# Seven products instead of eight for two more column groups of the projection and two more pairs of the second layer, and block sums taken from the transposes' banks

## The chip, the core and the metric

The kernel runs on one core of a Trainium2 chip. The metric is the time of one execution on the device, in microseconds (us): the median of 3 runs. The text calls TensorE PE (PEld is its weight load), VectorE DVE, ScalarE ACT, GpSimd POOL, and the engine that issues the transfers SP.

## What is computed

One transformer block on 2048 tokens of width 576: attention and a two-layer network stand side by side on the same normalized input, and both are added to `x`.

```python
def _A_ref(x, wqkv, wo):            # H = 32 heads of 18, W = 8 keys, every second token
    qkv = (lambda x, *d: x.transpose(*d))((x @ wqkv).reshape(B, S, 3, H, Dh), 2, 0, 3, 1, 4)
    ...
    logits = jnp.where(mask[None, None, :, :], logits, -1e9)
    attn = _softmax(logits, axis=-1)
    o = jnp.einsum("bhsw,bhswd->bhsd", attn, vg)
    return (lambda x, *d: x.transpose(*d))(o, 0, 2, 1, 3).reshape(B, S, D) @ wo

def _B_ref(x, w1, b1, w2):          # width F = 4608 between the layers, Mish
    h = jnp.einsum("bsd,df->bsf", x, w1) + b1
    ...
    return jnp.einsum("bsf,fd->bsd", act, w2)

xn = _layernorm(x, axis=-1)
return x + _A_ref(xn, A_wqkv, A_wo) + _B_ref(xn, B_w1, B_b1, B_w2)
```

## The kernel before, in words

**Number format.** Every operand of a matmul is split into a high part (a rounded copy, made by ACT) and a low part (the operand less its high part, made by DVE or POOL). A product of two operands is three matmuls: high by high, low by high, high by low. "Cast" is below the making of a high part, "low" that of a low part.

**Halves and blocks.** The tokens are worked off in two halves of 1024 (`hf`), each in two blocks of 512 (`b`), each of four tiles of 128 tokens (`jj`). Width 576 is four chunks of 128 and a rest of 64, which is stored twice. For each half come, in this order: normalization and transposition into the tiles `xt0` and `xt1` (`ln_transpose`, `transpose_split`: PE transposes into banks of PSUM, ACT and DVE split out of them); the projection to queries, keys and values in four column groups `g` of 432 columns; the two layers in 18 quads `q` of 256 hidden columns. The attention over the finished projection runs beside the quads on POOL, DVE and ACT, in 73 steps a half. The output projection by `wo` closes the program.

**Eight products or seven.** A product of 2 by 2 blocks takes eight block products, or seven if sums of blocks are made first. The sums of the input blocks are S1 to S4 (in the tiles `S0`, `S1`, `S2`, and S3 in place of A21), the differences of the weight blocks T1 to T4. Seven products were in use before in the first layer throughout (`m1_part`), in groups 2 and 3 of the second half (`z_part`, L502 to L577, 50 matmuls of 432 columns for each `jj`), in the second layer of the second half for `2 * OC` = 10 of its 18 quads (`p_item`, L949, seven items of 24 matmuls of 288 columns for two quads), and in the output projection. Groups 2 and 3 of the first half went through `qkv_item` (L416): 14 matmuls for each `g`, `b` and `jj`. The other eight quads of the second layer's second half went through `m2_cols` (L975): four chunks of 24 matmuls for each quad. The weight differences for the second half were prepared in the first: those of the second layer by `t_sum`, `t_high`, `t_low`, `t_keep` in quads 1 to 10, those of the projection by `z_load`, `z_sum`, `z_high`, `z_low`, `z_keep` from quad 10 on; both are written to DRAM and fetched later.

**Block sums.** `s_step` (L723) makes S1 to S4 on POOL, with three operations of 128x512 for S1 in each half of the columns `c`: A21 + A22 of the high parts, of the low parts, and the sum of the two.

**Order.** `plan` is a list of PE items; `add` appends one, `before(i, fn)` puts side work in front of item `i`, and each engine runs its instructions in the order in which the code issues them. Where the work stands is written by hand; the tables `MOVED`, `SUMS`, `AHEAD` shift single pieces of it, and `STEPS` holds the item at which each attention step stands. A tile waits for the readers of the buffer that it takes over. PSUM has four banks under the tag `h` and four under `out`.

**Start.** `first_item` interleaves the first four projection items with the transposes of their own tiles; its `mid` makes the root of tile 2's variance (ACT), then DVE's Newton step, then tile 3's statistics.

## Time and profile before

| | |
|---|---|
| median of 3 runs | 1104.5 us (1103.47, 1104.5, 1105.23) |
| the profiled execution's own time | 1103.77 us |
| its span (first to last instruction) | 1102.0 us |
| ACT busy | 503.7 us (46%), 927 instructions |
| DRAM traffic | read 162.16 MB, written 111.77 MB, mean 249 GB/s |
| matmuls of `qkv_item` (L439) | 672 of 432 columns |
| matmuls of `m2_cols` (L982) and `p_item` (L961) | 768 and 840 of 288 columns |

The page gives each engine's busy time, then the span in 40 slices, then the chain of waits, followed back from the last instruction. A window is a stretch of the span with each engine's busy time in it. A line of the timeline has the start, the duration, the engine, the code line, the tiles and, in brackets, the idle time before it with its releaser.

### The profile page before, as it was taken

The numbers are of one execution on the slowest core, as the hardware profiler recorded it, in microseconds if no ns is written. First come the engines' busy times: TensorE is split into PE (matmuls) and PEld (weight loads), VectorE is DVE, ScalarE is ACT, GpSimd is POOL, SyncE is SP. The second block draws the span as 40 slices with busy tenths as digits, with TensorE's granted clock in tenths as the row PEclk, the third lists the DMA queues.
The fourth block names the chain that finished last, engine by engine and source line by source line (L and its number), as shares of the span: only waits on it lengthen the run. The fifth ranks groups of instructions, "written<-read, shape, count | busy, mean of one in ns | idle before, by whom it ended". The sixth has DMA issues, their size and how long they took to land.

```text
span 1102.0 us, 18226 instructions
## 1 busy us (share of the span) xinstructions
PE 1095.1 (99%) x6526; PEld 1010.7 (92%) x6526; DVE 864.6 (78%) x1381; ACT 503.7 (46%) x927; POOL 800.9 (73%) x647
## 2 busy tenths in 40 slices
...
GB/s 204 283 312 302 256 344 224 249 264 261 259 281 211 287 252 306 260 257 227 171 307 301 226 337 341 241 218 221 207 240 185 180 219 201 239 309 198 250 218 139
DMA packets 181933, 275.12 MB, mean 250 GB/s; under 512 B 53426, under 2 KB 123860, under 8 KB 181844
## 3 DMA queue, kind: packets, MB, share of 16 engines
...
HBM read 162.16 MB, written 111.77 MB: 249 GB/s over the span
## 4 chain that ended last, share of the span: by engine, by line
PE 97%; DVE 1%; ACT 1%; POOL 0%; DMA 0%; issue 0%; SPq 0%; POOLq 0%
PE h L769 31%; PE po L869 21%; PE pq L439 11%; PE po L961 10%; PE po L982 9%; PE h L775 6%; PE o L1165 5%; PE z L537 4%; POOL act L821 0%; PE ta L163 0%; DMA acc<-in_x 0%; DVE st L200 0%; DVE accP L985 0%; PE tt L163 0%; DVE xt L170 0%
## 5 line engine op out<-in xcount | busy, mean ns | idle before, releaser
L869 PEld LDWEIGHTS po<-w,act 128*128 128x128 f32 x1728 | 236.3, 188 | 5.7 <-POOL act L821 0.4
L869 PE MATMUL po<-w,act 128*128 128x288 f32 x1728 | 240.6, 295 | 0.1
L627 POOL TENSOR_TENSOR pr<-q,kv 128x576 f32<-128x576 f32 x128 | 195.8, 1556 | 7.9 <-DMA q<-q_d 5.3
L666 POOL TENSOR_TENSOR pv<-L,kv 128x576 f32<-128x576 f32 x128 | 177.7, 1488 | 23.5 <-DVE L L659 12.9
L821 POOL TENSOR_TENSOR act<-c,act 128x512 fp32r<-128x512 f32 x75 | 103.2, 1376 | 113.0 <-ACT act L820 100.2
L439 PE MATMUL pq<-wq,xt 128*128 128x432 f32 x672 | 136.1, 360 | 0.9 <-ACT xt L169 0.6
L873 DVE TENSOR_TENSOR acc<-po,acc 128x288 f32<-128x288 f32 x288 | 117.2, 447 | 23.1 <-PE po L869 21.9
L439 PEld LDWEIGHTS pq<-wq,xt 128*128 128x128 f32 x672 | 125.0, 188 | 7.5 <-ACT xt L169 1.3
L961 PEld LDWEIGHTS po<-pw,u 128*128 128x128 f32 x840 | 114.9, 188 | 2.9 <-issue 0.2
L961 PE MATMUL po<-pw,u 128*128 128x288 f32 x840 | 116.8, 294 | 0.0
L815 ACT ACTIVATE c<-c,b1c 128x512 f32<-128x512 f32 x75 | 54.4, 725 | 129.4 <-DVE c L814 129.2
L769 PE MATMUL h<-xt,t 128*128 128x512 f32 x432 | 110.6, 391 | 0.2 <-DVE c L814 0.2
L769 PE MATMUL h<-S,t 128*128 128x512 f32 x432 | 110.4, 391 | 0.0
L982 PEld LDWEIGHTS po<-w,act 128*128 128x128 f32 x768 | 104.5, 188 | 2.7 <-DVE accP L985 0.7
L982 PE MATMUL po<-w,act 128*128 128x288 f32 x768 | 106.4, 295 | 0.1
L769 PE MATMUL h<-xt,wa 128*128 128x512 f32 x432 | 103.9, 389 | 0.0
L632 DVE TENSOR_REDUCE L<-pr 128x64 f32<-128x1152 f32 x64 | 85.6, 1340 | 19.6 <-POOL pr L627 19.5
L672 DVE TENSOR_REDUCE og<-pv 128x144 f32<-128x1152 f32 x64 | 85.9, 1344 | 18.6 <-POOL pv L666 18.6
L769 PEld LDWEIGHTS h<-xt,wa 128*128 128x128 f32 x432 | 80.9, 188 | 16.6
L803 ACT COPY c<-h 128x512 f32<-128x512 f32 x75 | 43.9, 586 | 108.2 <-PE h L775 62.2
L769 PEld LDWEIGHTS h<-xt,t 128*128 128x128 f32 x432 | 79.0, 188 | 15.3 <-DVE rt L814 0.5
L769 PEld LDWEIGHTS h<-S,t 128*128 128x128 f32 x432 | 77.9, 188 | 13.2 <-ACT rm L803 0.5
...
## 6 DMA issues: line engine op xcount, KB each, us to landing
...
```

Of the source, the lines that this page charges most:

```text
L439: nc.tensor.matmul(pq[:, 0:432], XT[:, xi, tok], wt[wi][:, hl, 0:432], start=i == 0, stop=i == len(seq) - 1)
L627: nc.gpsimd.tensor_tensor(out=pr[:, x:x + hh], in0=q[:, j0 + x:j0 + x + hh, None, :].to_broadcast([P, hh, W, CU]), in1=win(kt, 0, CU, j0 + ...
L632: nc.vector.tensor_reduce(L[:, k, j0:j0 + hj].rearrange("p j w h -> p (j w h)"), pr.rearrange("p j w (h d) -> p (j w h) d", h=2), axis=AX, ...
L666: nc.gpsimd.tensor_tensor(out=pr[:, x:x + hj].rearrange("p j d w -> p j w d"), in0=L[:, k, x:x + hj, :, h:h + 1].to_broadcast([P, hj, W, DH]),
L672: nc.vector.tensor_reduce(og[:, c0:c0 + DH, :].rearrange("p d j -> p j d"), pr, axis=AX, op=ALU.add)
L769: nc.tensor.matmul(ph, wt[:, wl, wk * P:(wk + 1) * P], X[:, xs, :], start=first and i == 0, stop=last and i == len(seq) - 1, skip_group_ch ...
L775: nc.tensor.matmul(ph, wt[:, wl, off * P:(off + 1) * P], X[:, xs, :], start=False, stop=wl == 1, skip_group_check=True)
L821: nc.gpsimd.tensor_tensor(out=a[:, 1, :], in0=t, in1=a[:, 0, :].bitcast(F32), op=ALU.subtract)
L869: nc.tensor.matmul(po, acts[hf, q, b, j][:, al, tok], done["w2", hf, 2 * q + j][:, wl, c * HC:(c + 1) * HC], start=i == 0, stop=i == 5)
L873: nc.vector.tensor_tensor(out=t, in0=po, in1=t, op=ALU.add)
L961: nc.tensor.matmul(po, units[e, k, qq][:, al, tok], w[:, qq, wl, :], start=i == 0, stop=i == 5)
L982: nc.tensor.matmul(po, acts[hf, q, b, j][:, al, tok], done["w2", hf, 2 * q + j][:, wl, c * HC:(c + 1) * HC], start=i == 0, stop=i == 5)
```

## The change

Five things are edited, and the order tables are written anew.

1. **Projection, first half, groups 2 and 3.** The 16 items of `qkv_item` go. In their place stand 14 items `y` (`za_part`), product by product in the order of `YORDER`: B11, B21, T2, T3, T4, T1, B22, each in two items of two `jj`. The last item of B22 stands inside quad 0, where the last `qkv_item` stood. The products that use B11, T2, T1 and B22 add up in one bank for each `jj` (four `out` banks for the whole stretch), B21 takes the four `h` banks, and T3 with T4 takes them over. ACT copies an intermediate state out of a bank, DVE adds another product to it. The raw weights (`za_load`) and their differences (`za_sum`, now on DVE) are made here; casts, lows and the way to DRAM (`za_high`, `za_low`, `za_keep`) too, for 16 tiles. So `z_load` to `z_keep` in quads 10 to 12 go. Block sums S1 to S3 of the first half are needed in this stretch, and their steps move ahead of it. The attention of the first half begins behind it.
2. **Second layer, second half.** `OC` goes from 5 to 6: twelve quads by `p_item`, six by `m2_cols`. `t_sum` to `t_keep` run for quads 11 and 12 too.
3. **A21 + A22.** `transpose_split` of block 1 has DVE add up the pairs in the bank, straight into the sum's tile; the three POOL operations for each `c` go, in both halves.
4. **Start.** The first half of tile 3's statistics stands between tile 2's root and its Newton step.
5. **Small moves.** The first block's products of the first chunk of quad 0 use the high parts first; the table for Mish is loaded in the projection; the loads of the second half's `x` stand six items later, the preparation of `wo` starts one quad further on and is spread over fewer items.

```diff
-OC = 5
+OC = 6
...
-STEPS = ((21, 22, 24, 26, 28, 30, 33, 38, 50, 51, 59, 61, 69, 71, 79, 81, 89, 92, 99, 104, 109, 110, 119, 121, 126, 128, 129,
...
+STEPS = ((36, 41, 47, 49, 53, 57, 63, 67, 70, 77, 78, 83, 85, 91, 95, 98, 105, 107, 111, 117, 123, 127, 130, 137, 139, 143,
...
+        if both is not None:
+            nc.vector.tensor_reduce(both, ta.rearrange("p (j k t) -> p k t j", j=2, k=2), axis=AX, op=ALU.add)
...
+    def half_stats(n, t):
+        if n not in half_st:
+            half_st[n] = sb.tile([P, 2, 6], F32, tag="st", bufs=4, name=f"st_{next(tpn)}"), []
+        st, ins = half_st[n]
+        c = len(ins)
+        ins.append(nc.vector.bn_stats(st[:, c, :], t[:, c * 288:(c + 1) * 288]))
...
+                half_stats(3, accs[0][3])
...
+        both = None
+        if b:
+            c, at_ = divmod(jj, 2)
+            if not at_:
+                s0[hf, c] = s_tmp(0)
+            both = s0[hf, c][:, :, at_ * P:(at_ + 1) * P]
+        transpose_split(xn, XTs[hf, b], jj * P, rem if b else None, (hf, b) == (1, 0) and jj < 3, both)
...
+    YHOME = {"B11": ("wb", "wb"), "B21": ("wb", "wc"), "R2": ("wc",), "R3": ("wc",), "T2": ("r3", "a0"),
+             "T3": ("a0", "a0"), "T4": ("a1", "a1"), "T1": ("a0", "a0"), "B22": ("a0", "a1")}
...
+    def za_sum(name, k):
...
-        nc.gpsimd.tensor_tensor(out=zraw[name, k], in0=zraw[x, k], in1=zraw[y, k], op=ALU.subtract)
+        nc.vector.tensor_tensor(out=zraw[name, k], in0=zraw[x, k], in1=zraw[y, k], op=ALU.subtract)
...
+    YORDER = ("B11", "B21", "T2", "T3", "T4", "T1", "B22")
...
+        to, add_ = {"B11": ((2, 0), 0), "B21": ((2, 0), 1), "T2": ((2, 1), 0), "T3": ((3, 1), 0), "T4": ((2, 1), 1),
+                    "T1": ((3, 1), 1), "B22": ((3, 0), 0)}[name]
...
+            if name == "B11":
+                yq["h1", jj] = ps.tile([P, 512], F32, tag="out", bufs=4, name=f"y1_{jj}")[:, 0:432]
+            elif name in ("B21", "T3"):
+                yq["h3", jj] = ps.tile([P, 512], F32, tag="h", bufs=4, name=f"y{name}_{jj}")[:, 0:432]
+            h = yq["h3" if name in ("B21", "T3", "T4") else "h1", jj]
+            seq = [(src[:, xs + k, tok], yw[name, k][:, wl]) for k in range(2) for xs, wl in ((hi, 0), (lo, 0), (hi, 1))]
+            if rest is not None:
+                seq += [(rest[0][:, rest[1], tok], yw[rest[2], 0][:, wl]) for wl in range(2)]
+            for i, (l, r_) in enumerate(seq):
+                nc.tensor.matmul(h, l, r_, start=i == 0 and name in ("B11", "B21", "T3"), stop=i == len(seq) - 1,
+                                 skip_group_check=True)
+            for d, v in ((kvs[:, :, jj, :], h[:, 0:288].rearrange("p (u c) -> p u c", u=2 * UQ)),
+                         (qs[:, :, jj, :], h[:, 288:432].rearrange("p (u c) -> p u c", u=UQ))):
+                if add_:
+                    nc.vector.tensor_tensor(out=d, in0=v, in1=d, op=ALU.add)
+                else:
+                    nc.scalar.copy(d, v)
...
-        t = stmp[k] = s_tmp(k)
-        if k == 0:
-            u = s_tmp("u")
-            gp(t, p["A21"][0], p["A22"][0], ALU.add)
-            gp(u, p["A21"][1], p["A22"][1], ALU.add)
-            gp(t, t, u, ALU.add)
-        elif k == 1:
+        t = stmp[k] = s_tmp(k) if k else s0[hf, c]
+        if k == 1:
             gp(t, stmp[0], p["A11"][0], ALU.subtract)
             gp(t, t, p["A11"][1], ALU.subtract)
         elif k == 2:
             gp(t, p["A12"][0], stmp[1], ALU.subtract)
             gp(t, t, p["A12"][1], ALU.add)
-        else:
+        elif k == 3:
...
-            for g, b in ((2, 0), (2, 1), (3, 1), (3, 0)):
-                for jj in range(JB - 1 if (g, b) == (3, 0) else JB):
-                    qi(hf, g, b, jj)
+            for n in range(len(YORDER)):
+                for half in range(2):
+                    if (n, half) != (len(YORDER) - 1, 1):
+                        yi(n, half)
...
+    z0 = at["y", 0, 0]
+    for name, k, lead in (("B11", 0, 12), ("B11", 1, 12), ("B12", 0, 11), ("R2", 0, 11), ("B21", 0, 10), ("B22", 0, 10),
+                          ("B21", 1, 9), ("B12", 1, 8), ("B22", 1, 8)):
+        before(z0 - lead, lambda name=name, k=k: za_load(name, k))
+    before(z0 + 1, lambda: za_load("R3"))
+    for name, k, d in (("T3", 0, -5), ("T1", 0, -5), ("T2", 0, -4), ("T3", 1, -1), ("T1", 1, -1), ("T2", 1, 0), ("T4", 0, 0),
+                       ("T4", 1, 1)):
+        before(z0 + d, lambda name=name, k=k: za_sum(name, k))
+    for name, k, d in (("B11", 0, -4), ("B11", 1, -3), ("B21", 0, -2), ("B21", 1, -1), ("R2", 0, -1), ("T2", 0, -3), ("T2", 1, 1),
+                       ("T3", 0, 1), ("T3", 1, 1), ("T4", 0, 2), ("T4", 1, 2), ("R3", 0, 5), ("T1", 0, 8), ("T1", 1, 8),
+                       ("B22", 0, 9), ("B22", 1, 10)):
+        before(z0 + d, lambda name=name, k=k: za_high(name, k))
+        before(z0 + d + (name[0] != "B" or name == "B22"), lambda name=name, k=k: za_low(name, k))
+        before(z0 + d + 4, lambda name=name, k=k: za_keep(name, k))
+    plan[z0 + 2][1].append(lambda: nc.scalar.preload_act_table_set("mish"))
...
-    i = spot(0, 2 * OC, 6)
...
-    i = spot(1, 2 * OC + 3, 0)
+    i = spot(1, 2 * OC + 2, 0)
...
-        k = i + 10 + (2, 5, 8, 12, 15, 19, 23, 27, 31)[n]
+        k = i + 8 + (0, 2, 5, 8, 11, 14, 17, 20, 23)[n]
```

PE where group 2 begins (item 20 of the plan in both). Before: `pq_0_<b>_<g>_<jj>` is the bank of a projection item, with weights of the group's five chunks:

```order
L439 MATMUL pq_0_0_2_0_802<-wq_0_10_653,xt_0_0_227 128x432 x3
L439 MATMUL pq_0_0_2_0_802<-wq_0_11_677,xt_0_0_227 128x432 x3
L439 MATMUL pq_0_0_2_0_802<-wq_0_12_707,xt_0_0_227 128x432 x3
L439 MATMUL pq_0_0_2_0_802<-wq_0_13_737,xt_0_0_227 128x432 x3
L439 MATMUL pq_0_0_2_0_802<-wq_0_14_766,xt_0_0_227 128x432 x2
```

Now, at the end of B21 and the start of T2: `y1_<jj>` are the `out` banks, `yB21_<jj>` the `h` banks, `yw_..._<k>` the weights of a product in its two chunks:

```order
L559 MATMUL yB21_3_934<-yw_B21_0_709,xt_0_0_227 128x432 x3
L559 MATMUL yB21_3_934<-yw_B21_1_786,xt_0_0_227 128x432 x3
L559 MATMUL yB21_3_934<-yw_R2_0_789,xt_0_0_227 128x432 x2
L559 MATMUL y1_0_821<-yw_T2_0_739,S1_0_656 128x432 x3
L559 MATMUL y1_0_821<-yw_T2_1_847,S1_0_656 128x432 x3
```

An item of 14 matmuls with one group's weights became six or eight matmuls of one product, and the first product on a block sum (S1) stands 56 matmuls behind the start of the group.

DVE from the last split of block 1 on. Before, the lows of group 2's weights and of the block sums alternate with attention (`L`):

```order
L346 TENSOR_TENSOR wq_0_10_653<-rwq_10_597,wq_0_10_653 128x432
L346 TENSOR_TENSOR wq_0_11_677<-rwq_11_619,wq_0_11_677 128x432
L346 TENSOR_TENSOR wq_0_12_707<-rwq_12_634,wq_0_12_707 128x432
L346 TENSOR_TENSOR wq_0_13_737<-rwq_13_656,wq_0_13_737 128x432
L346 TENSOR_TENSOR wq_0_14_766<-rwq_14_680,wq_0_14_766 128x432
L755 TENSOR_TENSOR S0_0_682<-s_0_16_683,S0_0_682 128x2x256
L346 TENSOR_TENSOR wq_0_15_821<-rwq_15_740,wq_0_15_821 128x432
```

Now, the twelve operations up to B11's second low, which PE's item 20 reads (`yT3_0<-yB22_0,yB12_0` is a difference, `yw_...` a low):

```order
L513 TENSOR_TENSOR yT3_0_681<-yB22_0_575,yB12_0_555 128x432
L513 TENSOR_TENSOR yB12_0_555<-yB12_0_555,yB11_0_529 128x432
L820 TENSOR_TENSOR S0_0_620<-s_0_12_513,S0_0_620 128x2x256
L513 TENSOR_TENSOR yT2_0_704<-yB22_0_575,yB12_0_555 128x432
L522 TENSOR_TENSOR yw_B11_0_706<-yB11_0_529,yw_B11_0_706 128x432
L513 TENSOR_TENSOR yT3_1_735<-yB22_1_618,yB12_1_616 128x432
L820 TENSOR_TENSOR S1_0_656<-s_1_18_657,S1_0_656 128x2x256
L820 TENSOR_TENSOR S2_0_660<-s_2_19_661,S2_0_660 128x2x256
L522 TENSOR_TENSOR yw_B21_0_709<-yB21_0_573,yw_B21_0_709 128x432
L522 TENSOR_TENSOR yw_T2_0_739<-yT2_0_704,yw_T2_0_739 128x432
L513 TENSOR_TENSOR yB12_1_616<-yB12_1_616,yB11_1_531 128x432
L522 TENSOR_TENSOR yw_B11_1_737<-yB11_1_531,yw_B11_1_737 128x432
```

Behind them stand, ahead of DVE's first addition out of a bank of B21, thirteen more of the same kinds: five lows of weights up to T3's, five lows of block sums (S3's both columns last) and three differences. No attention step stands in between any more.

PE in the second half where quad 10 of the second layer was read, a chunk of `m2_cols` before (`w2_...` are the weights as they are, `act_...` the activations of one block of tokens):

```order
L982 MATMUL po_1_10_1_0_0_0_9886<-w2_1_22_9431,act_1_1_20_9788 128x288 x3
L982 MATMUL po_1_10_1_0_0_0_9886<-w2_1_23_9456,act_1_1_21_9821 128x288 x3
L982 MATMUL po_1_10_1_0_0_1_9894<-w2_1_22_9431,act_1_1_20_9788 128x288 x3
L982 MATMUL po_1_10_1_0_0_1_9894<-w2_1_23_9456,act_1_1_21_9821 128x288 x3
L982 MATMUL po_1_10_1_0_1_0_9902<-w2_1_22_9431,act_1_1_20_9788 128x288 x3
L982 MATMUL po_1_10_1_0_1_0_9902<-w2_1_23_9456,act_1_1_21_9821 128x288 x3
```

Now, the first of the sixth set's seven items (`u_5_0_<qq>` is the prepared left side, `pw_5_0` the weights of the product):

```order
L1028 MATMUL po_5_0_0_0_9976<-pw_5_0_9802,u_5_0_0_9868 128x288 x3
L1028 MATMUL po_5_0_0_0_9976<-pw_5_0_9802,u_5_0_1_9948 128x288 x3
L1028 MATMUL po_5_0_0_1_9984<-pw_5_0_9802,u_5_0_0_9868 128x288 x3
L1028 MATMUL po_5_0_0_1_9984<-pw_5_0_9802,u_5_0_1_9948 128x288 x3
L1028 MATMUL po_5_0_1_0_9992<-pw_5_0_9802,u_5_0_0_9868 128x288 x3
L1028 MATMUL po_5_0_1_0_9992<-pw_5_0_9802,u_5_0_1_9948 128x288 x3
```

A chunk and an item have the same 24 matmuls of 288 columns; for two quads there were eight chunks and there are seven items, and each item waits for a left side that ACT, DVE and POOL have made.

274 lines of the change are left out of this document (146 added, 128 removed), and 17 rows, old and new, of tables (STEPS, i).

## The prediction

> **What bounds the kernel now.** I read the page's busy times first, then PE's waits, then the chain of waits, and last the windows and timelines of the places that the change touches.
>
> ```profile
> span 1102.0 us, 18226 instructions
> ...
> PE 1095.1 (99%) x6526; PEld 1010.7 (92%) x6526; DVE 864.6 (78%) x1381; ACT 503.7 (46%) x927; POOL 800.9 (73%) x647
> ```
>
> PE is idle for 1102.0 - 1095.1 = 6.9 us of the span. A share of 99% alone doesn't prove a bound, since a matmul's end is modelled; PE's waits do (line waited for, total, times, longest):
>
> ```profile
> PE warm L153 <- POOL ident masks.py:199: 1.3, 1, 1.3
> PE ta L163 <- ACT xn L268: 0.9, 2, 0.5
> PE pq L439 <- ACT xt L169: 0.6, 1, 0.6
> PE pq L439 <- POOL wq L1287: 0.2, 1, 0.2
> PE h L769 <- DVE c L814: 0.2, 1, 0.2
> ```
>
> All the waits together are 3.2 us, nearly all of them in the start. From then on PE never waits for long, so a matmul less is its issue interval less, as long as nothing new comes late. The chain of waits gives these intervals (start, length, line, matmuls), for 432 columns in the projection and in the seven-product form, and for 288 columns in `p_item` and `m2_cols`:
>
> ```profile
> 42.37 57.74 PE pq L439 x294
> 585.81 37.75 PE z L537 x192
> 653.13 3.17 PE po L961 x24
> 1028.68 15.90 PE po L982 x120
> ```
>
> 57.74 / 294 = 0.1964 us, 37.75 / 192 = 0.1966 us: the seven-product form costs no more for each matmul. 3.17 / 24 = 0.132 us and 15.90 / 120 = 0.1325 us: the same holds in the second layer.
>
> **The change part by part.** *Fewer matmuls.* Groups 2 and 3 of the first half had 16 items of 14 = 224 matmuls; seven products have 50 for each of four `jj`, 200. That is 24 x 0.1964 = 4.71 us less. Two quads of the second layer had 8 x 24 = 192 matmuls and have 7 x 24 = 168: 24 x 0.1325 = 3.18 us less. Both lie on PE's path: 7.89 us. The number of matmuls stands in the code, so that the change saves none is excluded; only lateness can take it back.
>
> *The start.* PE stands still before tile 3's transposes, behind the chain statistics, root, Newton, normalization:
>
> ```profile
> 17.74 0.66 PE L163 MATMUL ta<-ident,xn 128*128 128x128 f32 x4 [0.43 <-ACT xn L268]
> ```
>
> ```profile
> 11.97 0.27 DVE L255 TENSOR_SCALAR y<-rs,ve 128x1 f32<-128x1 f32 x1 [0.51 <-ACT rs L248]
> ...
> 14.02 0.82 DVE L200 BATCH_NORM_STATS2 st<-acc 128x6 f32<-128x288 f32 x2
> ```
>
> Half of the 0.82 us moves into DVE's gap of 0.51 us, so the chain ends 0.41 us earlier and takes nearly all of the 0.43 us away. What is late next is the split of that tile, on ACT. Gain 0 to 0.43 us; I take 0.3. A loss is excluded unless tile 3's data land after 11.5 us, which no row shows.
>
> *The sums from the banks.* Eight reductions of 128x512 to 128x256 are new on DVE. The trace has none of this size; the nearest rows, one line of the page and one of the groups of DVE, are
>
> ```profile
> L632 DVE TENSOR_REDUCE L<-pr 128x64 f32<-128x1152 f32 x64 | 85.6, 1340 | 19.6 <-POOL pr L627 19.5
> ```
>
> ```profile
> L647 DVE TENSOR_REDUCE m<-L 128x32 f32<-128x256 f32 x16 | 6.7, 420 | 0.5
> ```
>
> Bounds 0.42 and 1.34 us; by the number of inputs 0.42 + 256 / 896 x 0.92 = 0.68 us, nearer to the short one. Each stands between the split of a bank and its release. The tightest bank goes from the second transposition to the third:
>
> ```profile
> 36.04 0.69 DVE L170 TENSOR_TENSOR xt<-ta,xt 128x512 fp32r<-128x512 f32 x1 [1.23 <-ACT xt L169]
> ```
>
> ```profile
> 38.58 0.27 PE L164 MATMUL tb<-ident,xn 128*128 128x128 f32 x1
> ```
>
> The split ends at 36.73, the reduction would at 37.41, and PE wants the bank at 38.58: 1.17 us of cover; even at 1.34 us PE would wait only 0.17 us. Cost 0. POOL loses twelve operations of the 1.33 us that the L719 row below shows, 16 us; PE's waits name none of them.
>
> *The product stretch.* This is the part with a price. With the chain's row, item 20 starts 84 matmuls after 42.37: 58.9 us. PE reads B11's second low with its sixth matmul, at 59.9. B11, B21 and T2 are 80 matmuls, so T3 takes over B21's first bank at 58.9 + 15.7 = 74.6. Two chains must keep these dates.
>
> First the loads. SP's issues before (start, length, line, count) and their landing:
>
> ```profile
> 24.81 10.63 SPq L364 DMA_DIRECT2D kept_wq<-wq  x10
> ...
> 37.88 3.50 SPq L287 DMA_DIRECT2D rwq<-in_wq  x4
> ```
>
> ```profile
> rwq<-in_wq SPq DMA_DIRECT2D x7, 216.0 KB, 4.9
> ```
>
> Behind the ten kept weights (35.4) eight issues lead up to B22's first part, at 3.50 / 4 = 0.88 us each: 42.4, landed 4.9 us later at 47.3. Then DVE's twelve operations, nine of 432 columns and three of 512, run up to B11's second low. DVE's timeline shows what such operations take, each kind without and with POOL at work, and POOL's timeline what POOL did beside the two long ones:
>
> ```profile
> 62.72 0.61 DVE L346 TENSOR_TENSOR wq<-rwq,wq 128x432 fp32r<-128x432 f32 x1 [2.55 <-ACT wq L345]
> 63.24 0.69 DVE L755 TENSOR_TENSOR S<-s,S 128x512 fp32r<-128x512 f32 x1
> ...
> 73.71 1.57 DVE L346 TENSOR_TENSOR wq<-rwq,wq 128x432 fp32r<-128x432 f32 x1
> 75.20 1.92 DVE L755 TENSOR_TENSOR S<-s,S 128x512 fp32r<-128x512 f32 x1
> ```
>
> ```profile
> 72.15 2.66 POOL L719 TENSOR_TENSOR s<-s,xt 128x512 f32<-128x512 f32 x2
> 74.77 3.64 POOL L627 TENSOR_TENSOR pr<-q,kv 128x576 f32<-128x576 f32 x2
> ```
>
> Alone the twelve take 9 x 0.61 + 3 x 0.69 = 7.6 us (54.9), all beside POOL 9 x 1.57 + 3 x 1.92 = 19.9 us (67.2). POOL has about four operations of 1.33 us in this time, each of which lengthens one of DVE's by about 1.0 us: 58.9, that is 1.0 us ahead of PE. Thirteen more, eight of 432 and five of 512, lead up to the first addition out of B21's bank: 8.3 us alone, 22.2 us beside POOL, and with POOL's six operations for S3 14.3 us: 73.2. The addition itself is in the groups of DVE:
>
> ```profile
> L550 DVE TENSOR_TENSOR zkv<-z,zkv 128x288 f32<-128x288 f32 x12 | 5.5, 456 | 10.0 <-PE z L537 9.7 <-ACT S L751 0.3
> ...
> L550 DVE TENSOR_TENSOR zqs<-z,zqs 128x144 f32<-128x144 f32 x12 | 3.6, 298 | 0.0
> ```
>
> 0.456 + 0.298 = 0.75 us, so the bank is free at 74.0, 0.6 us ahead. In sum 25 operations have 74.6 - 0.75 - 47.3 = 26.5 us, 1.06 us each, and I expect (15.9 + 10) / 25 = 1.04. Behind the late operation the bank additions are queued, and PE waits for these. Cost between 0 and 67.2 - 59.9 = 7.3, then 67.2 + 22.2 + 0.75 - (74.6 + 7.3) = 8.2 more, 15.5 us in all. A gain is excluded, since the matmuls saved are counted already. The nearest row is the mixed one: in the window before, where POOL was busy for most of the time, such operations were
>
> ```profile
> L346 DVE TENSOR_TENSOR wq<-rwq,wq 128x432 fp32r<-128x432 f32 x10 | 9.3, 930 | 15.6 <-ACT wq L345 13.0 <-issue 2.4
> L755 DVE TENSOR_TENSOR S<-s,S 128x512 fp32r<-128x512 f32 x6 | 8.9, 1483 | 0.0
> ```
>
> With 17 of 0.93 and 8 of 1.48 the mean is 1.11 us, 0.05 x 25 = 1.2 us late. Between that and on time I take 0.7 us.
>
> *Attention and the second half.* The attention's first steps leave the stretch and go into the quads, which before had this room (window, length, then busy times of PE, PEld, DVE, ACT, POOL):
>
> ```profile
> 384.00:432.00 48.00, 48.00 (x293) 44.06 (x292) 43.79 (x63) 22.37 (x39) 44.02 (x35) 1.00 0.81 283
> 660.00:868.00 208.00, 207.95 (x1249) 189.94 (x1248) 167.73 (x256) 90.11 (x148) 157.67 (x111) 1.00 0.70 237
> ```
>
> The first is the fullest stretch of the first half, two quads with 4.2 us of DVE's time free. Three steps more come into sixteen quads, about 1.34 us of DVE each, 0.25 us a quad, and the second-half projection's preparation leaves quads 10 to 12: cost 0; without that room a microsecond costs one. The second window is that of ten quads with `p_item`, in which PE lost 0.05 us of 208. Two quads more of the same kind cost nothing there; each item that came late would cost its lateness. The table load, the order within one chunk, `x`'s later loads and `wo`'s preparation have the idle ACT and SP as cover: 0.
>
> Sum against the profiled execution: 1103.77 - 7.89 - 0.3 + 0.7 = 1096.3 us. The median of the runs is 0.73 us above that execution, which lies inside their spread; half of it added gives 1096.6 us.
>
> **The rivals.** *The product stretch goes at DVE's pace in part.* With a mean of 1.22 us, 25 operations are 30.5 us, 4.0 us late, and the time is 1096.6 - 0.7 + 4.0 = 1099.9. For it speak the 1.92 us row and the thin cover; against it that POOL has only about ten operations there, 13.3 us, and attention is gone.
>
> *DVE and POOL shut each other out for the whole stretch (the slower side).* With every operation at its long row 15.5 us are lost: 1096.6 - 0.7 + 15.5 = 1111.4. It makes the kernel slower by more than 0.2% from about 11 us of lateness on, that is a mean of (26.5 + 11) / 25 = 1.50 us. Against it: POOL would have to be at work without a gap, and its operations for S3 write into buffers that DVE's own lows must release first. The Trainium skill (SBUF — State Buffer, section "Who interferes with whom") states that a DVE instruction with two SBUF inputs and a GpSimd instruction that reads SBUF exclude each other for the whole instruction, whoever starts first; the 0.61 and 1.57 us rows agree with that.
>
> *The left sides of the second layer's new items come late.* If each of the seven waits 0.45 us, the 3.18 us are gone: 1099.8. For it: the last set now stands next to the splitting of quad 12. Against it: 0.05 us lost in ten quads.
>
> **How the numbers follow.** Forecast 0.64, first rival 0.17, slower rival 0.06, third rival 0.09; 0.04 for a loss of the whole gain by something that I do not see. A part of the first rival ends within 0.2% (2.2 us, about what a measurement of this kernel can tell): faster 0.86, same 0.07, slower 0.07. Low end: the fastest run, 1103.47 - 7.89 - 0.43 = 1095.1, rounded to 1095.0. High end: the first and the third rival with 1.1 us over: 1101.0. Outside lie the slower rival, the unseen loss and the tails, 0.2 or less.
>
> **What would show it.** In the profile after, the page must have 48 matmuls fewer; the chain's intervals must stay at 0.196 and 0.132 us; tile 3's transposes start without the 0.43 us; PE's waits must show less than 1.5 us on the lines of `za_part`. The first rival shows there as waits for DVE, on B11's second low or on T3's bank; the third as waits of `p_item` for ACT, DVE or POOL in quads 12 and 13. Wrong I am if PE waits for over 5 us in one place, or if a line that I called covered (a bank of the transposes, quad 0's weights, the last quads) stands among PE's waits with over 1 us.

## The result, and the profile after

The changed kernel takes 1113.0 us (median of five, 1110.8 to 1114.2) beside 1104.3 for the kernel before: ratio 1.0076, 95% interval 1.0061 to 1.0090. It is 8.7 us slower, where 7.9 us faster was forecast. The profiled execution's own time is 1110.76 us, the fastest of the five.

The page's busy times of the kernel after:

```profile
span 1109.0 us, 18148 instructions
...
PE 1094.4 (99%) x6478; PEld 1005.4 (91%) x6478; DVE 874.6 (79%) x1433; ACT 508.7 (46%) x935; POOL 780.1 (70%) x635
```

The 48 matmuls are gone (6526 to 6478), yet PE is busy for only 0.7 us less: busy time, in which every matmul counts until its modelled end, hides what became slower. PE's idle time rose from 6.9 to 14.6 us. PE's waits of the kernel after (line waited for, total, times, longest):

```profile
PE po L1049 <- DVE accP L1052: 2.9, 1, 2.9
PE po L1028 <- DMA pw<-kept_T: 1.5, 1, 1.5
PE h L834 <- ACT t L365: 1.5, 1, 1.5
PE warm L156 <- POOL ident masks.py:199: 1.3, 1, 1.3
PE z L607 <- ACT zqs L616: 0.9, 1, 0.9
PE ta L166 <- ACT xn L282: 0.9, 2, 0.5
PE z L607 <- DVE zqs L620: 0.8, 1, 0.8
PE pq L459 <- ACT xt L172: 0.7, 1, 0.7
PE h L834 <- DVE t L366: 0.7, 1, 0.7
```

None is on the lines of `za_part`. The chain of waits passes the new stretch at the forecast intervals (4.72 / 24 = 0.197 us), and the first item of quad 0 starts at 94.7 us of the span instead of 99.9:

```profile
58.83 4.72 PE y L559 x24
63.55 6.28 PE yB L559 x32
69.83 4.69 PE y L559 x24
74.52 10.96 PE yT L559 x56
85.48 6.30 PE y L559 x32
```

So the gain was there, and was lost behind it. 26 matmuls fewer stand ahead of quad 0 now, 5.1 us, and two more inside it, since the last item of B22 has 16 where the last `qkv_item` had 14. I cut the span where the first matmul of an item starts, with the same cuts in each kernel (us of each stretch; "quads 0, 1" ends where quad 2 begins, "z" runs from the first matmul of groups 2 and 3 of the second half to its quad 0; the e-runs are explained below):

| stretch | before | after | e1 | e10 | e14 | e16 | e18 |
|---|---|---|---|---|---|---|---|
| up to quad 0 | 99.94 | 94.74 | 94.65 | 95.50 | 95.09 | 94.62 | 100.16 |
| quads 0, 1 | 38.64 | 41.69 | 41.48 | 42.95 | 42.99 | 41.56 | 38.63 |
| quads 2 to 9 | 192.65 | 193.95 | 193.48 | 193.15 | 201.85 | 197.23 | 192.65 |
| quads 10 to 16 | 168.62 | 169.45 | 168.62 | 168.75 | 169.11 | 174.07 | 180.20 |
| quad 17 and the second half's first groups | 85.79 | 85.95 | 85.87 | 85.86 | 85.86 | 85.80 | 85.79 |
| z | 37.75 | 39.93 | 40.87 | 39.47 | 37.73 | 38.17 | 37.75 |
| second half, quads 0 to 13 | 311.19 | 311.37 | 309.20 | 309.27 | 309.58 | 310.09 | 309.23 |
| quad 14 to the output projection | 109.83 | 114.50 | 115.22 | 111.48 | 110.13 | 110.23 | 110.23 |

By z the whole lead is gone (z starts at 585.64 us before, at 585.78 after), and 7 us more follow. Where PE's clock went to half for 3.41 us, a stretch holds 1.7 us of that: in after and e1 the last one (in e1 6.83 us, so up to 3.4), in e10 quad 1, in e14 quad 1 and quads 2 to 9, in e16 quads 2 to 9 and 10 to 16. Four kinds of loss can be seen.

*The last chunks.* DVE's timeline around the longest wait, then POOL's, then two windows (length, then busy times of PE, PEld, DVE, ACT, POOL, then the clock):

```profile
962.06 1.35 DVE L702 TENSOR_REDUCE L<-pr 128x64 f32<-128x1152 f32 x1 [1.89 <-POOL pr L697]
963.33 8.01 DVE L1133 TENSOR_TENSOR raw_T<-raw_T,woh_T 128x576 fp32r<-128x576 f32 x2
971.27 0.68 DVE L879 TENSOR_TENSOR c<-h,c 128x512 f32<-128x512 f32 x1
```

```profile
963.25 2.79 POOL L697 TENSOR_TENSOR pr<-q,kv 128x576 f32<-128x576 f32 x2
966.02 1.28 POOL L886 TENSOR_TENSOR act<-mn,act 128x512 fp32r<-128x512 f32 x1
967.26 2.79 POOL L697 TENSOR_TENSOR pr<-q,kv 128x576 f32<-128x576 f32 x2
```

```profile
970.00:975.00 5.00, 2.05 (x13) 1.59 (x13) 5.00 (x9) 2.97 (x5) 1.35 (x2) 0.99 0.71 203
975.00:980.00 5.00, 5.00 (x23) 4.73 (x22) 4.83 (x11) 1.13 (x2) 0.00 (x0) 0.67 0.97 333
```

The first of the two lows of `wo`'s differences (L1133) takes 7.3 us, as long as POOL works without a gap. PE's `c` and `accP` are queued behind it: PE stands still for 2.9 us. Then its clock goes to half for 3.41 us (0.67 in the mean of the second window): 1.7 us more.

*A transfer.* SP's issues before the 1.5 us wait for `pw`:

```profile
887.32 4.63 SPq L771 DMA_DIRECT2D o_d<-oT  x4
892.07 1.41 SPq L996 DMA_DIRECT2D pw<-kept_T  x1
```

An attention step's results hold SP's queue for 4.63 us, and the weights of a sixth-set product are issued late by that. This is read from the timeline; no run moves these issues alone.

*Attention in quad 1 and in z.* DVE in quad 1 (the 1.5 and 0.7 us waits), then POOL and ACT in z (the 0.9 and 0.8 us waits):

```profile
107.76 1.35 DVE L702 TENSOR_REDUCE L<-pr 128x64 f32<-128x1152 f32 x1 [3.14 <-POOL pr L697]
109.03 0.87 DVE L366 TENSOR_TENSOR wc<-rw,wc 128x384 fp32r<-128x384 f32 x1
109.83 1.78 DVE L366 TENSOR_TENSOR t<-tt,t 128x512 fp32r<-128x512 f32 x1
```

```profile
582.52 5.74 POOL L736 TENSOR_TENSOR pv<-L,kv 128x576 f32<-128x576 f32 x4 [3.07 <-ACT S L816]
588.07 1.32 POOL L789 TENSOR_TENSOR s<-xt,s 128x512 f32<-128x512 f32 x1
```

```profile
590.80 0.62 ACT L816 CAST S<-s 128x512 fp32r<-128x512 f32 x1 [3.07 <-POOL s L789]
```

In both, a step of the attention stands in a queue ahead of what PE needs: in quad 1 a reduction that waits 3.14 us for POOL, ahead of the weights' lows; in z two steps close together on POOL, ahead of a block sum whose cast holds up ACT's copies out of the banks. Before, eight steps were done when quad 1 began, after only one: seven have to go somewhere else. By `STEPS`, quads 1 to 17 take three of them (46 steps for 43), the second half's first groups two and z two (nine for seven).

*Something that no wait shows.* In quads 10 to 16 PE waits for nothing, and still each takes 169.45 / 7 = 24.21 us instead of 24.09. The chain of waits of before, then of after, at the same twelve matmuls:

```profile
186.91 2.72 PE h L769 x12
```

```profile
185.02 2.79 PE h L834 x12
```

2.79 / 12 = 0.2325 us against 0.2267. These are products of `xt` and `wa`; the mean over all 576 of that kind, from one start to the next in the trace's records, is 226.9 ns before and 232.9 after: 3.5 us. The products of other operands keep their intervals to 1.4 ns. One thing differs in these: the tile `r3`, first used ahead of `wa` now, has 3456 bytes in a partition, 13.5 times 256, and has moved `wa0` and `wa1` in SBUF by 128 bytes against the other operands, modulo 256.

### The profile page after: what moved, and what is told of

It is laid out like the page before. It is cut to its first block, busy times and chain, and to the rows that moved or that the text cites. A ratio compares the mean times of both kernels' runs of the same rounds, so it can differ in the third digit from the quotient of the medians.

```text
span 1109.0 us, 18148 instructions
## 1 busy us (share of the span) xinstructions
PE 1094.4 (99%) x6478; PEld 1005.4 (91%) x6478; DVE 874.6 (79%) x1433; ACT 508.7 (46%) x935; POOL 780.1 (70%) x635
## 4 chain that ended last, share of the span: by engine, by line
PE 92%; DMA 2%; DVE 2%; issue 1%; POOL 1%; SPq 1%; ACT 0%; DVEq 0%; ACTq 0%; POOLq 0%
PE h L834 29%; PE po L936 21%; PE po L1028 12%; PE pq L459 7%; PE po L1049 6%; PE h L840 6%; PE o L1232 5%; PE z L607 4%; PE y L559 1%; PE yT L559 1%; PE yB L559 1%; DMA pw<-kept_T 1%; DMA kept_yB<-yw_B 1%; DMA w<-kept_w 1%; PE ta L166 0%
## 5 line engine op out<-in xcount | busy, mean ns | idle before, releaser
L936 PEld LDWEIGHTS po<-w,act 128*128 128x128 f32 x1728 | 236.5, 188 | 5.7
L936 PE MATMUL po<-w,act 128*128 128x288 f32 x1728 | 240.6, 295 | 0.0
L886 POOL TENSOR_TENSOR act<-c,act 128x512 fp32r<-128x512 f32 x69 | 93.7, 1358 | 99.6 <-ACT act L885 94.1
L1028 PEld LDWEIGHTS po<-pw,u 128*128 128x128 f32 x1008 | 138.3, 188 | 5.5 <-issue 1.9
L1028 PE MATMUL po<-pw,u 128*128 128x288 f32 x1008 | 140.7, 295 | 1.5 <-DMA pw<-kept_T 1.5
L834 PE MATMUL h<-xt,wa 128*128 128x512 f32 x432 | 106.2, 395 | 0.0
L880 ACT ACTIVATE c<-c,b1c 128x512 f32<-128x512 f32 x69 | 50.0, 725 | 121.5 <-DVE c L879 121.3
L459 PE MATMUL pq<-wq,xt 128*128 128x432 f32 x448 | 91.8, 362 | 0.8 <-ACT xt L172 0.7
L459 PEld LDWEIGHTS pq<-wq,xt 128*128 128x128 f32 x448 | 83.0, 188 | 5.6 <-ACT xt L172 1.1
L1049 PEld LDWEIGHTS po<-w,act 128*128 128x128 f32 x576 | 79.9, 191 | 5.0 <-DVE accP L1052 3.4
L1049 PE MATMUL po<-w,act 128*128 128x288 f32 x576 | 81.2, 298 | 2.9 <-DVE accP L1052 2.9
L868 ACT COPY c<-h 128x512 f32<-128x512 f32 x69 | 40.4, 585 | 86.5 <-PE h L840 43.5
```

The source lines that it names most:

```text
L459: nc.tensor.matmul(pq[:, 0:432], XT[:, xi, tok], wt[wi][:, hl, 0:432], start=i == 0, stop=i == len(seq) - 1)
L834: nc.tensor.matmul(ph, wt[:, wl, wk * P:(wk + 1) * P], X[:, xs, :], start=first and i == 0, stop=last and i == len(seq) - 1, skip_group_ch ...
L886: nc.gpsimd.tensor_tensor(out=a[:, 1, :], in0=t, in1=a[:, 0, :].bitcast(F32), op=ALU.subtract)
L936: nc.tensor.matmul(po, acts[hf, q, b, j][:, al, tok], done["w2", hf, 2 * q + j][:, wl, c * HC:(c + 1) * HC], start=i == 0, stop=i == 5)
L1028: nc.tensor.matmul(po, units[e, k, qq][:, al, tok], w[:, qq, wl, :], start=i == 0, stop=i == 5)
L1049: nc.tensor.matmul(po, acts[hf, q, b, j][:, al, tok], done["w2", hf, 2 * q + j][:, wl, c * HC:(c + 1) * HC], start=i == 0, stop=i == 5)
```

## The experiments

Each run is compared with the kernel before on the same chip (1103.9 to 1104.4 us). Two runs from different chips are best compared by their ratios, which are given beside the medians where the two disagree. "e1" stands for the kernel after with the first edit, on which most of the later ones build.

### The address of wa (e1, e2, e11)

e1 reserves the two `wa` tiles ahead of `r3` in the kernel after, e2 reserves `r3` ahead of `wa` in the kernel before. Nothing that is computed changes.

```diff
 e1, in za_high of the kernel after
+        if not yw:
+            for n in range(2):
+                sb.tile([P, 2, 5 * P], F32R, tag=f"wa{n}", bufs=1, name=f"wa_first_{n}")
 e2, in new() of the kernel before
+        if (kind, hf, i) == ("wa", 0, 0):
+            sb.tile([P, 2 * 432], F32R, tag="r3", bufs=1, name="r3_first")
```

> The changed kernel with one thing put back: the two first-layer weight tiles wa0 and wa1 are reserved ahead of the r3 tile, so that they start at an address that leaves 64 modulo 256 bytes, as before the change, and not 192. No instruction is added, removed or moved. Theory A (the place of wa in SBUF): the products with wa take 0.227 us again where they took 0.228 to 0.241, a first-half quad takes 24.08 us again for 24.21, and 36 quads give back 4 to 5 us: 1108 to 1109 us for 1113. Rival B (those intervals are long for another reason, such as the traffic of the new order): 1113 us, and the intervals stay.

> The kernel before, with the r3 tile reserved ahead of the first wa tile: wa0 and wa1 then start at 192 modulo 256 bytes, as in the changed kernel, and nothing else is altered. Theory A: the products with wa get 0.006 us longer on average, a first-half quad takes 24.2 us for 24.08, and the whole is 4 to 5 us slower, 1108 to 1109 us for 1104.3. Rival B: 1104.3 us.

e1: 1107.6 us, ratio 1.0021 (1.0009 to 1.0032), 5.4 us less than after (6.1 by the ratios). e2: 1108.6 us, ratio 1.0037 (1.0023 to 1.0050), 4.2 us more than before. The chain of e1, then of e2:

```profile
281.61 2.72 PE h L837 x12
```

```profile
283.93 2.79 PE h L771 x12
```

Both ways round the interval follows the address (the mean over all 576 is 226.9 ns in e1, 232.9 in e2), and so does the time: the theory holds. In e2's profile, which is of its slowest execution, one stall of 1.8 us is not the address. e11 measures it by itself: 24 products of 512 columns for each distance of the weights from the moving operand, in steps of 32 bytes, twice.

```diff
+                o = 8 * ph + 128 * (k % 6)
+                nc.tensor.matmul(hs[r], wts[:, o:o + P], big[:, k % 5], start=k == 0, stop=k == 23)
```

> A measurement by itself, without the kernel's work (the output is filled with zeros). First, 512-column products with the weights at 16 addresses, 32 bytes apart, and the moving operand where it is: theory A gives 0.227 us a product at weights' offsets of 0 and 256 bytes from the moving operand's place, and 0.230 to 0.241 at 128; without it all are alike. Then VectorE adds two tiles of 576 columns, started one to four short operations after a chain of 0, 1, 2, 3, 5 or 8 additions of GpSimd: theory G gives, for both sources in SBUF, 0.7 us without GpSimd and in some of the cases the whole rest of the chain (up to 11 us for eight), and for a source in PSUM or a reduction the same time whatever the chain; under rival M (one instruction of GpSimd at most) no more than 2.1 us.

Mean distance from one start to the next, worked out from the trace's records: 226.7 ns at 0 and 256 bytes; 229.3 at 192; 233.1 to 233.9 at 32, 64, 96, 128, 160 and 224; the same beyond 256. The kernel's shift of 128 bytes is one of the dear ones. In e11 the two tiles both lie at 128 modulo 256, in the kernels `xt` lies at 64, and a distance of 0 is the fast one in both: so it is the distance that counts, not the weights' own address. GpSimd and DVE were at work beside these products at every distance, and the two rounds agree within 0.1 ns. The Trainium skill (SBUF — State Buffer, section "Who interferes with whom") says that PE never waits on anyone; the 6 to 7 ns here lie between PE's own two operands, which that sentence doesn't cover. e11 also held a first form of e13's test, in which DVE began 0.19 us ahead of GpSimd; nothing follows from that part.

### Other dates for what came late (e3, e4, e6, e7, e8, e9, e12)

The remaining theory was that single attention steps and sums stand badly. e3 moves the reduction of quad 1 and steps in z and in the second half of the kernel after and leaves four entries of `SUMS` out; e4 is e3 with e1's edit; e6 moves one step of the second half from item 396 to the end; e7 moves quad 1's reduction four items later and a cast one earlier; e8 is e6 and e7 with z's steps at every second place; e9 lets the first half's attention begin at item 45 instead of 36, without the first entry of `SUMS`.

```diff
 e3
-SUMS = {(0, 0): (38, 0),
+SUMS = {(0, 0): (42, 0),
-  ... 233, 235, 236, 238, 240, 241, 243, 245, ...   -  ... 357, 361, ...   -  ... 392, 394, 396, ...
+  ... 233, 235, 237, 239, 241, 242, 244, 245, ...   +  ... 357, 359, 361, ...   +  ... 392, 396, ...
 e6
-  ... 394, 396, 398, ... 425))
+  ... 394, 398, ... 425, 426))
 e7
-SUMS = {(0, 0): (38, 0),                  -  t1=i + 10
+SUMS = {(0, 0): (42, 0),                  +  t1=i + 9
 e9
-STEPS = ((36, 41, 47, 49, 53, 57, ...
+STEPS = ((45, 47, 49, 51, 53, 57, ...
```

> The changed kernel with some dates of the attention altered in its order tables, wa left where it is: the first block's first reduction comes four places later (after quad 1's second sum weights), the steps around the second half's first products get two places each again, and one step is brought forward into the quads in which GpSimd has time (the eleventh), so that none falls at the place where GpSimd ran without a gap. Theory C (the losses are waits in the queues of DVE, GpSimd and SyncE behind the attention's new dates): PE's waits of 2.2 us at quad 1, 1.7 us in the first products of the second half, 1.5 us in the thirteenth quad's products and 2.9 us at the last chunks' adds go, and with the last one the stretch at the halved clock (1.7 us): 8 to 10 us, 1103 to 1105 us for 1113. Rival D (the waits come from the work itself, and show up elsewhere once the dates move): at most 3 us, 1110 to 1113 us.

> Both at once: wa back at its old place modulo 256 bytes, and the altered dates of the attention. Theories A and C add up: 4 to 5 us and 8 to 10 us, so 1098 to 1101 us for 1113, under the kernel before. If only A holds 1108 to 1109, if only C 1103 to 1105, if neither 1113.

> The changed kernel with wa put back and one thing more: the attention's step at place 396 and those behind it come one step later, so that GpSimd's queue in the fifteenth quad has no second pair of key products behind the first. Theory G (a VectorE operation with both sources in SBUF gets no turn as long as GpSimd goes from one instruction to the next without a pause, and PE's clock is halved behind the wait): the low of a wo weight takes under 2.5 us where it took 7.3, PE's wait of 3.2 us at the last chunks and the 6.8 us at half clock go, 6.6 us less than the profile of the kernel with wa put back: 1101 to 1103 us. Rival H (GpSimd is simply full there, and the wait comes with the next operation): 1106 to 1109 us, with a wait of 2 us or more between 900 and 1000 us.

> The changed kernel with wa put back and two dates altered at quad 1: the attention's first reduction four places later, and the fourth weight cast of quad 1 one place earlier. Theory C for this place alone (VectorE stands for 3 us behind the attention's first products): PE's waits of 2.3 us at quad 1's second part fall under 0.5 us, and the whole is 1.5 to 2.3 us less than with wa put back: 1105.3 to 1106.2 us. Rival D (the cover is gone there, and another wait takes the place): 1107 to 1108 us with a wait of over 1 us between 105 and 140 us.

> All of it: wa put back, the gap in GpSimd's queue in the fifteenth quad, quad 1's two dates, and the steps around the second half's first products spaced as in the run of the altered dates. If G and C hold: 6.6 us and 2 us, and 1 us at the first products, less than with wa put back: 1098 to 1099 us, 5 us under the kernel before. If H and D hold: 1106 to 1108 us.

> The changed kernel with wa put back, and the attention's start moved nine places back: its first five steps at 45, 47, 49, 51, 53 for 36, 41, 47, 49, 53, so that its loads of k, q and v are issued behind the loads and writes of quad 1's weights. Theory K (the waits of 2.3 us at quad 1 are the DMA's: between 100 and 120 us its engines are full with the products' kept weights, quad 0's and quad 1's weights and the attention's loads at once): the waits fall under 0.8 us and the stretch from quad 1 to quad 2 from 27.0 to 25.3 us: 1105.5 to 1106 us for 1107.6. Rival L (the casts and lows of quad 1's weights are too many for ScalarE and VectorE there): 27 us as before, 1107 to 1108 us.

| | us | ratio to before | what went | what came in its place |
|---|---|---|---|---|
| e3 | 1116.9 | 1.0101 (1.0078 to 1.0125) | quad 1: 2.2 to 0.7 us | 5.0 us from 924 on, half clock for 6.83 us from 926 on |
| e4 | 1111.2 | 1.0054 (1.0034 to 1.0075) | as e3, and the address | as e3, and 1.7 us at 122 |
| e6 | 1106.4 | 1.0023 (1.0013 to 1.0033) | L1133's long low: 7.3 to 4.6 us | half clock for 3.41 us in quad 1, behind waits that e1 has too |
| e7 | 1107.4 | 1.0031 (1.0020 to 1.0042) | quad 1's two waits | 2.1 us at 121, half clock for 3.41 us |
| e8 | 1106.1 | 1.0023 (1.0006 to 1.0040) | L1133's as in e6 | 2.1 us, as in e7 |
| e9 | 1109.1 | 1.0044 (1.0032 to 1.0056) | quad 1: 25.2 us, against 27.0 in e1 | 2.0 us at about 150, half clock |

PE's longest wait in e3, in e7 beside the old one at the last chunks, and in e9, in this order:

```profile
PE po L1049 <- DVE accP L1052: 5.0, 1, 5.0
```

```profile
PE po L1052 <- DVE accP L1055: 3.3, 1, 3.3
PE po L939 <- DVE acc L943: 2.1, 1, 2.1
```

```profile
PE po L939 <- DVE acc L943: 2.0, 1, 2.0
```

The rival wins: a step that leaves one place makes DVE late at the next, and e3 is slower than even its rival had it. e6's step, which goes behind everything, gives 1.2 us by the medians, but nothing by the ratios (1.0023, e1 1.0021).

### The lows of wo's differences off DVE (e10, e12)

In e10 four lows go to GpSimd (e1 otherwise); e12 is e10 with e9's start and z's even steps.

```diff
-        nc.vector.tensor_tensor(out=src.bitcast(F32R), in0=src, in1=h.bitcast(F32), op=ALU.subtract)
+        (nc.gpsimd if name[0] == "T" else nc.vector).tensor_tensor(out=src.bitcast(F32R), in0=src, ...
```

> The changed kernel with wa put back, and the lows of four wo weights (T1 to T4) made by GpSimd instead of VectorE. Theory G (the VectorE operation that gets no turn between GpSimd's instructions is what holds PE at the last chunks): no VectorE operation over 3 us near 960 us, PE's wait of 3.2 us and the 6.8 us at half clock behind it go: 1101 to 1103 us for 1107.6. Rival H (GpSimd is the bound there): GpSimd gets 5.6 us more to do, the wait stays at 3 us or more: 1107 to 1110 us.

> wa put back, the attention's start moved nine places back, the steps around the second half's first products spaced as in the run of the altered dates, and the lows of four wo weights on GpSimd. If K and G hold: 1.7 us, 1 us and 6 us less than with wa put back: 1098 to 1099.5 us, 5 us under the kernel before. If L and H hold: 1106 to 1109 us.

e10: 1104.6 us, ratio 1.0003 (0.9993 to 1.0012), 3.0 us less than e1 by the medians and 2.0 by the ratios; that lies between the theory's range and the rival's. e12: 1105.7, ratio 1.0014 (1.0004 to 1.0024). What the four lows took on DVE, one line each of before, after and e6 (shortest, median, longest in ns):

```profile
L1066 DVE TENSOR_TENSOR raw_T<-raw_T,woh_T x4: 748/1426/1707, 944.1 to 968.2; 128x576 fp32r<-128x576 f32 x4
```

```profile
L1133 DVE TENSOR_TENSOR raw_T<-raw_T,woh_T x4: 744/940/7344, 963.3 to 985.3; 128x576 fp32r<-128x576 f32 x4
```

```profile
L1136 DVE TENSOR_TENSOR raw_T<-raw_T,woh_T x4: 747/754/4600, 964.3 to 981.9; 128x576 fp32r<-128x576 f32 x4
```

The wait at the last chunks goes from 3.2 us in one to 1.6 in two, the clock stays full there, and the stretch from quad 14 on takes 111.48 us instead of 115.22:

```profile
PE po L1052 <- DVE accP L1055: 1.6, 2, 0.9
```

That the lows on DVE caused this loss is thereby shown. Their length alone does not do it: in e3 the same low takes 7.77 us, and PE does not wait behind it. e10 is the best version found, and only equals the kernel before.

### What holds a DVE operation up for 7 us (e13, e17)

Such operations are no trait of the new dates. Before has one of 5.25 us, with POOL at work beside it, and PE does not wait behind it; e10 has another low of `wo` of 7.68 us, and PE waits 0.7 us behind it. In this order:

```profile
883.79 5.25 DVE L649 TENSOR_TENSOR L<-L,m 128x256 f32<-128x256 f32 x1
```

```profile
984.33 7.68 DVE L1136 TENSOR_TENSOR rB<-rB,woh_B 128x576 fp32r<-128x576 f32 x1
```

Two kernels only measure: in e13 a DVE operation (two inputs from SBUF, one from PSUM and one from SBUF, or a reduction) meets up to eight GpSimd additions without a gap; in e17 48 lows meet additions and the attention's products.

```diff
 e13
+                for k in range(n):
+                    nc.gpsimd.tensor_tensor(out=gc, in0=ga, in1=gb, op=ALU.add)
+                for k in range(pre):
+                    nc.vector.tensor_reduce(vb[:, 8:16], pt.rearrange("p (a b) -> p a b", a=8), axis=AX, op=ALU.add)
+                    ...
+                    nc.vector.tensor_tensor(out=vd, in0=va, in1=vc, op=ALU.add)
```

> The measurement of VectorE's turns once more, without the kernel's work (the output is filled with zeros): in the first one VectorE's operation began 0.19 us ahead of GpSimd's chain in nearly all cases. Now it stands behind one to four reductions out of PSUM of 0.6 us, and so begins inside the chain of 1, 2, 3, 5 or 8 additions. Theory G: with both sources in SBUF it ends 0.6 us behind the last addition of the chain in some cases, up to 10 us for eight; with a source in PSUM, and as a reduction, it takes 0.69 and 0.75 us always. Rival M: it gets the next gap between two additions always, at most 2.1 us.

> VectorE's turns measured with the kernel's own kinds of instruction, without the kernel's work (the output is filled with zeros): GpSimd runs without a pause through sixty additions, then through pairs of key products, then through lows of activations, then through a mixture of them; VectorE runs beside it a reduction of 1152 columns and the low of a weight, in place, over and over. Theory G: in the mixture or among the key products some lows wait for several of GpSimd's instructions (3 us and more). Rival M: every low gets its turn at the next end of an instruction of GpSimd, 2.1 us at most, and the 4.5 to 7.8 us of the kernel have a cause that this does not hold.

The operation with two inputs from SBUF in e13, the low in e17:

```profile
L185 DVE TENSOR_TENSOR vd<-va,vc x20: 748/1644/1936, 25.7 to 102.2; 128x576 f32<-128x576 f32 x20
```

```profile
L221 DVE TENSOR_TENSOR lox<-lox,hix x48: 742/1376/1837, 27.4 to 172.5; 128x576 fp32r<-128x576 f32 x48
```

Never over 1.94 us: DVE gets its turn when GpSimd's instruction ends. With its second input in PSUM it took 0.68 us each time, as a reduction 0.74. The Trainium skill (SBUF — State Buffer, section "Who interferes with whom") states that a DVE instruction with two SBUF inputs contends with a GpSimd instruction that reads SBUF; this agrees with both runs for one instruction, but makes no 7.3 us of it. In e17 DVE was through before GpSimd came to the activations' lows and the mixture of kinds, so these weren't met. Why single operations took 4.6 to 7.9 us in the kernels stays open.

### The parts by themselves (e5, e18)

e5 is the kernel after with `OC` back at 5, the second half in before's order and e1's edit: the first half's part alone. e18 is the kernel before with `OC = 6`, after's dates in the second half, the second half's projection weights prepared in quads 12 to 16 (at 0.7 of the spacing) instead of 10 to 15, and e10's lows: the second layer's part alone.

```diff
 e5                 e18
-OC = 6             -OC = 5
+OC = 5             +OC = 6
 e18
-    i = spot(0, 2 * OC, 6)
+    i = spot(0, 12, 6)
-                d = 28 * k + (2 * n if n < 10 else (19, 20, 22, 23, 25, 26, 27)[n - 10])
+                d = int(0.7 * (28 * k + (2 * n if n < 10 else (19, 20, 22, 23, 25, 26, 27)[n - 10])))
```

> One part of the change alone: the first half's seven products, the sums from the transposes' banks and the new dates of the first half, with the second layer's pairs back at ten, the wo sums back at their old dates, and the whole second half in the order of before; wa lies at its old place modulo 256 bytes. Theory E (the second-layer part costs more than its 24 matmuls give, at the last chunks, and the products' part gives 4.7 us less the waits of quad 1 and of the first products of the second half, some 5 us): 1103 to 1106 us, under the changed kernel with wa put back (1107.6), and no wait over 1 us after 640 us. Rival F (the loss lies in the products' part throughout, and the second layer gives its 3.2 us): 1109 to 1111 us.

> This is the kernel before with the second layer's part alone: twelve quads by seven products instead of ten, its dates in the second half taken from the kernel after, the preparation of the second half's projection moved from quads 10 to 15 into quads 12 to 16 (at 0.7 of the old spacing), and the lows of wo's differences on GpSimd as in the tenth run. The first half's projection stays with eight products and the attention begins at 61 us as before. Theory (the loss of the change lies in the attention that the first half's product stretch pushes into the quads, and in the last chunks): quad 1 and the first products of the second half stay as before (24.5 us for quad 1, 9.8 for the first to the second tile of the second half), the second layer gives 2.1 to 3.2 us, and the time is 1101.0 to 1102.5. Rival R (the quads have no room for the preparations either, since the seven-product form of two more quads brings its own work to DVE): waits of the first layer for DVE in quads 11 to 16, the gain is gone, 1103.5 to 1107.

e5: 1109.8 us, ratio 1.0047 (1.0032 to 1.0062). Rival F's time came: the first half's part, which should give 4.7 us, costs 5.6 by itself; beside e1 the second layer gives 2.2 of its 3.2 (2.9 by the ratios). But a wait that neither theory had stands at the last chunks, behind a low of `wo` that is long with before's dates too:

```profile
PE po L969 <- DVE accP L972: 2.8, 1, 2.8
```

```profile
998.39 4.72 DVE L1053 TENSOR_TENSOR rB<-rB,woh_B 128x576 fp32r<-128x576 f32 x1
```

So the long lows need neither the second layer's part nor `wo`'s new dates. Another 1.7 us of e5's profile are half clock behind a wait of 2.5 us in z. e18: 1115.2 us, ratio 1.0110 (1.0091 to 1.0129). My theory was wrong on its time: quads 10 to 16 lose 11.6 us. But quad 1, z and all else of the first half are as before to 0.2 us, and from z to the output projection e18 is 1.6 us faster than before. e18's waits, and a window in quad 14:

```profile
PE h L690 <- DVE c L735: 5.1, 4, 2.3
PE po L790 <- DVE acc L794: 3.9, 3, 2.2
```

```profile
443.00:456.00 13.00, 10.20 (x64) 9.33 (x65) 12.57 (x22) 5.16 (x10) 4.70 (x4) 1.00 0.68 243
```

DVE is busy without a gap there, POOL for a third of the time, and PE waits. So the parts hang together: the second layer's takes the room on DVE that the projection's part frees in quads 10 to 15, and that part needs room for seven attention steps. How much of e18's loss is its own denser preparation was not tried.

### The old attention dates behind the new stretch (e14, e15, e16)

If the shifted steps are the cause, z must be as before once they stand as before at the end, and the price must appear where the extra steps go. The last 19 steps of the first half stand as before in all three; the extra steps go to items 73, 88 and 101 (quads 4, 5 and 7) in e14, e15 also begins as late as items 40 and 44, and e16 puts them at 113, 140 and 150 (quads 8, 11 and 12). All are e10 otherwise, less the entries of `SUMS` that belonged to the old dates: five in e14 and e15, so that sums move there too, and one in e16, where another is renumbered.

```diff
 e14
-STEPS = ((36, 41, ... 70, 77, 78, 83, 85, 91, 95, 98, 105, ... 216, 217, 219, 221, 223, 227, 228, 230, ... 255),
+STEPS = ((36, 41, ... 70, 73, 77, 78, 83, 85, 88, 91, 95, 98, 101, 105, ... 219, 221, 225, 227, 229, 231, ... 256),
 e16
+STEPS = ((36, 41, ... 111, 113, ... 139, 140, ... 147, 150, ... 219, 221, 225, 227, 229, 231, ... 256),
```

> The kernel with wa put back and four lows on GpSimd, with the attention's first-half steps changed: three more of them between the third and the sixth quad, so that the last nineteen stand where they stood before the change, one in every second place. Theory N (the 2.3 us lost around the second half's first products are GpSimd's and SyncE's queues, in which the attention is three steps behind where it was): from the first product to the next tile's 9.8 to 10.5 us for 11.0 to 12.3, and the whole 1 to 2 us less than 1104.6: 1102.5 to 1103.6 us. Rival O (the weights that are fetched there come late by themselves): 1104 to 1105 us, waits for the DMA of the last kept weights as before.

> As the run with the steps as before, with the attention's first two steps at 40 and 44 for 36 and 41 and its first reduction at 42. Theory K in a milder form: its loads come four places later, quad 1's waits fall from 2.3 to about 1 us, and no new wait comes at the adds behind it: 1101 to 1102.5 us. Rival P (whatever is moved there, the backlog of DMA and VectorE comes out as one wait of 2 us between 108 and 160 us): the same as without it, 1102.5 to 1104.6 us.

> The run with wa put back and four lows on GpSimd, with the last nineteen steps of the attention's first half where they stood before the change, as in the run with the steps as before, but the three steps that this needs spread over the ninth, twelfth and thirteenth quad instead of the fifth to eighth. Theory N: from the first product of the second half to the next tile's 9.8 us again for 11.0, and if VectorE has room in those three quads, 1.3 to 2.5 us less than 1104.6: 1102.1 to 1103.3 us. Rival Q (VectorE has no room for a step more in any quad of the first half): a wait of 1 to 3 us for its adds in each of the three, 1105 to 1110 us.

e14: 1111.5 us, ratio 1.0065 (1.0038 to 1.0092). e15: 1112.0, 1.0065 (1.0046 to 1.0083), with 9.0 us of waits for `c`, 7.4 of them in quads 2 to 9. e16: 1110.3, 1.0048 (1.0033 to 1.0063). z takes 37.73 us in e14, where before takes 37.75: that its loss is the attention's dates is shown. But 8.7 us are lost in quads 2 to 9 (e16: 4.1 there, 5.3 in quads 10 to 16, against e10), each time with 1.7 us of half clock in it. PE's longest waits of e14 and of e16, then a window of e14:

```profile
PE h L836 <- DVE c L881: 6.3, 5, 3.4
```

```profile
PE h L837 <- DVE c L882: 5.7, 4, 3.1
```

```profile
220.00:240.00 20.00, 16.64 (x97) 14.97 (x96) 19.80 (x37) 9.28 (x14) 11.67 (x10) 0.91 0.75 251
```

DVE works for 19.80 of 20 us in e14, while over a whole quad it has two us free: the step, the weights' lows and the differences of one quad fall together.

## Why the prediction was wrong

*Fewer matmuls* (-7.89): right. The counts and intervals came as stated, but the intervals only for 432 and 288 columns; that the 512-column products keep theirs was taken without saying so.

*Product stretch* (+0.7): right in its working, and on the safe side. The 25 operations took 1.05 us each, where 1.04 was expected; they began at 44.7 us for 47.3, so B11's second low was done at 58.3 us (58.9 expected) and the first bank of B21 free at 71.6 (74.0). Quad 0 begins 5.20 us earlier; no wait names DVE there, so both rivals on the stretch fall. *Bank reductions* (0): right, no wait names them; each took 0.68 us, as estimated.

*The start* (-0.3): it came and did not last. Tile 3's transposes begin at 17.44 us for 17.74, though PE, which is there earlier, still waits 0.41 us for them; at 38.1 us 0.04 us of the gain are left. Where it went was not followed up.

*Attention and the second half* (0): this is the step that failed. It divided DVE's free time over two quads, 4.2 us, by three steps spread evenly over sixteen quads. Waits come from what stands ahead of PE's work in a queue within some 10 us, not from the mean; and the steps that had to move were seven: three went into the quads, as it said, but four behind them, two of these into z, where it priced nothing. The profile showed what that costs in quad 1 (2.2 us of waits; quads 0 and 1 are 3.05 us longer, with the address and the two matmuls that moved into quad 0) and z (+2.18); e14 showed that z's loss goes when the steps stand as before, and e3, e7, e9 and e14 to e16 that no date tried for these steps costs clearly less. The preparation whose room it counted on had stood in quads 10 to 15 (its lows on DVE from 366.9 to 474.5 us), not 10 to 12. That "two quads more of the same kind cost nothing there" did not hold for the transfers: `pw`, 1.5 us.

*`wo`'s preparation* (0, with the idle ACT and SP as cover): wrong. Its lows run on DVE, not on ACT and SP; one met POOL without a gap, 2.9 us of wait and 1.7 us of clock. Taking four of them off DVE gives 3.0 us by the medians (e10). That the new dates made it so is not shown: e5 has such a wait at the old ones.

*Not in the prediction at all:* the address of `wa`, 3.5 us by the intervals, 4.2 and 5.4 us by the times of e2 and e1; and the half clock behind a wait.

The sum for the profiled execution: 1109.0 - 1102.0 + 7.89 = 14.9 us were lost behind what the fewer matmuls gave. Address 3.5, quad 1 2.2, z 2.2, last chunks 2.9 + 1.7, `pw` 1.5: 14.0. The other 0.9 us, net, are in pieces too small to name. The third rival (left sides late) did not come here: the 1.5 us wait at its place is for the weights; in e6, e8 and e9 PE does wait for `u`, 1.8 to 2.6 us. The prediction's own sign of being wrong, a covered line with over 1 us among PE's waits, came with `accP` in the last quads; `pw` and `t` in quad 1, over 1 us too, it had not listed.
